# The scatters of the last tokens' list entries placed behind the second early slot's list read and gathers on GpSimd

## Chip, cores, metric

One core of one Trainium2 chip. The metric is device microseconds of one execution, the median over runs.

## What is computed

Three stages on 4608 tokens of 512 values: packed attention (32 pack rows attend to each sequence, then the queries attend to the packs), a mixture of 8 experts in which every token goes to one expert, and a dense two-layer MLP. The part that this change touches is the second:

```python
e_idx = np.argmax(logits, axis=1)
for e in range(E):
    mask = e_idx == e
    h = np.maximum(x[mask] @ w1[e], 0.0)
    out[mask] = gate_w[mask, None] * (h @ w2[e])
```

## The kernel before

**Stages.** The program has two parts, each an order of instructions that a small planner (`Sched`) writes down before anything runs. The first part holds the attention of four batch pairs and, overlapped with its end, the first two expert slots and the fetching of the third slot's rows; the second part (behind a branch, line 1917) holds the third to tenth slot and the nine blocks of the dense MLP.

**Tokens to lists.** When a batch pair's attention output is done, `route` (line 755 on) stores the rows to the DRAM tensor `xs` (lines 806 and 809, on SyncE's queue), chooses an expert for each token on VectorE, and writes the token numbers into per-expert lists in the DRAM tensor `lst`. That write is `send` and `scatter`: per group of 128 tokens one indirect DMA on GpSimd (line 157, `lst<-ids,idx`) with a small memset ahead of it (line 156). A pair has 9 groups. The fourth and last pair is routed in three pieces of 4, 4 and 1 groups; these nine are the "scatters of the last tokens".

**Slots.** A slot is up to 470 tokens of one expert. The first two slots are "early": the first is filled from the tokens of the first two pairs, the second from those of the first three, so neither needs the last pair's list entries. `whole_gather` fills a slot: a list read on SyncE (line 1529, `tok<-lst`), then four indirect gathers on GpSimd (line 1532, `nat<-xs,tok`) into a buffer `nat` of which there is one. `whole_rows` transposes that buffer on TensorE in four sets of four (line 1551, `ft<-ident,nat`), and ScalarE and VectorE split each set into two parts (lines 1556 and 1559). `slot` then runs 8 weight chunks, each a first matmul of 12 pieces (line 1366, `h<-xT,war`) and a second of 12 (line 1674, `o<-g,wbr`). A chunk's weights are loaded by SyncE into one of two `raw` buffers (lines 1417 and 1421) and split on ScalarE (line 1441) and VectorE (line 1447) into a ring of three.

The third slot is an ordinary one and needs every list entry. Its number comes from `finalize` on VectorE (lines 1225 to 1270), its list read and gathers stand in the same two lines, and `slot_list` (line 1583, `st<-lst`) reads the fourth slot's list just behind.

**What sets the order.** `Sched.run` walks through time with estimated durations and always emits the instruction that could start first, by priority where several could. Each engine executes its instructions in the order of emission. The Tile framework adds the semaphores: a read of `lst` waits for every scatter emitted ahead of it, and a scatter emitted behind a read waits for that read. In the trace below "the first group" of gathers are the four of the first early slot, "the second" those of the second early slot, "the third" those of the third slot.

Of the kernel before, what the change touches and what calls it, by code (L numbers as in the profile page):

```python
# [28 lines left out]
NJ = 9  # L29
# [19 lines left out]
class Sched:  # L49
# [12 lines left out]
    def add(self, eng, dur, fn, w=(), r=(), hold=(), prio=0.0, lat=None, deps=(), after=0.0):  # L62
        o = Op()
        o.eng, o.dur, o.fn, o.prio, o.end, o.after = eng, dur, fn, prio, None, after
        o.lat = self.LAT.get(eng, 170.0) if lat is None else lat
        o.deps = list(deps)
        for b in r:
            o.deps += b.writers
        o.bufs = list({id(b): b for b in (*w, *r, *hold)}.values())
        for b in w:  # L70
            b.writers.append(o)
        for b in o.bufs:
            o.deps += b.gate
            b.left += 1
        self.ops.append(o)
        return o
# [12 lines left out]
    def ready(self, o, t):  # L89
        t = max(t, o.after)  # L90
        for d in o.deps:
            if d.end is None:
                return None
            t = max(t, d.end + d.lat)
        need = {}
        for b in o.bufs:
            if b.t is None:
                g = self.given.setdefault(b.key, [])
                k = len(g) + need.get(b.key, 0)
                if b.fifo and b.i != k:  # L100
                    return None
                need[b.key] = need.get(b.key, 0) + 1
                if k >= b.n:
                    p = g[k - b.n]
                    if p.left:
                        return None
                    t = max(t, p.done + 150.0)
        return t
# [1088 lines left out]
def finalize(tc, c, S, pool, tr, prio):  # L1197
# [67 lines left out]
    def taken():  # L1265
        v.tensor_tensor(sel, c["take"], oh.unsqueeze(1).to_broadcast([P, 3, G]), ALU.mult)
        v.tensor_reduce(res, sel, AX.X, ALU.add)
        v.tensor_scalar(add, slot, float(W), None, ALU.mult)
        v.tensor_copy(c["res"][:, 0:1], res[:, 0:1])
        v.tensor_scalar(c["res"][:, 1:3], res[:, 1:3], add, None, ALU.add)  # L1270
# [11 lines left out]
def pad(tc, ctx, n, **kw):  # L1282

    pool = ctx.enter_context(tc.tile_pool(name=f"pad{n}", bufs=1, **kw))
    pool.tile([P, n // 4], F32, name=f"pad_{n}")


class FFN:
# [354 lines left out]
    def slot(self, i, p0, xT, ereg, ready=(), raws=()):  # L1643
# [3 lines left out]
        step = 24 * MM * W / 512  # L1647
        os = self.outs()
        ws = list(ready)
        for fc in range(len(ws), NC1):  # L1650
            raw = raws[fc] if fc < len(raws) else None
# [220 lines left out]
def first_slot(tc, ctx, pctx, own, S, F, T):  # L1872

    def users(*keys):
        return [o for o in S.ops if any(b.key in keys for b in o.bufs)]

    def main():
        own.close()  # L1880
        pad(tc, ctx, 480, side="right")
        F.open(ctx, ("main",), side="right")
        F.open(ctx, ("ps_h",), side="right")

    def psum():
        pctx.close()
        F.open(ctx, ("ps_o",))

    F.gates["main"] = F.gates["ps_h"] = [S.swap(users(*KV_KEYS), main)]
    xT = F.whole_rows(F.xrows, T - 40000 + SHIFT["T0"])  # L1890
    swap = F.c["psum"]
    swap.fn, swap.deps = psum, users("tr", "sc", "xo")
    F.gates["ps_o"] = F.gates["ps_t"] = [swap]
    F.tr_of = None
    T += SHIFT["T5"]
    F.slot(-1, T, xT, [], raws=F.raws)
    for k, (chosen, F.stores, F.sends) in enumerate(F.later, 2):
        e = F.expert(-k, T - 15000, deps=[chosen])
        xT = F.whole_rows(F.whole_gather(-k, T - 12000, e), T)
        T += PER  # L1900
        F.slot(-k, T, xT, e)
    F.stores, F.sends = F.c["stores"], F.c["sends"]
    tables = finalize(tc, F.c, S, F.tables, F.tr, 20000.0)
    e = F.expert(NMORE, T - 10000, deps=[tables])
    xT = F.whole_rows(F.whole_gather(NMORE, T - 8000, e), T + 5000)
    ready = [F.moe_chunk(NMORE, fc, T + PER + (fc - 3) * 24 * MM, e) for fc in range(2)]
    raws = [F.moe_raw(NMORE, fc, T + PER + (fc - 3) * 24 * MM, e) for fc in (2, 3)]
    e = F.expert(NMORE + 1, T + 25000, deps=[tables])
    return xT, ready, raws, F.slot_list(NMORE + 1, T + 26000, e)


def slots_and_mlp(tc, ctx, F, xT, ready, raws, lists):
    nc, c = tc.nc, F.c
    shift = NE_ * NC1 % RING
# [60 lines left out]
def build(tc, ins, out):  # L1975
    nc = tc.nc
    with ExitStack() as ctx, tc.manual_schedule():
        pool = ctx.enter_context(tc.tile_pool(name="dram", bufs=1, space=DRAM))
        xs = pool.tile([NT, DM], F32, name="xs")
        lst = pool.tile([LIST, 2], I32, name="lst")  # L1980
        order = pool.tile([WIDE, 2], I32, name="order")
        yT = pool.tile([DM, WIDE], F32, name="yT")
        tab = ctx.enter_context(tc.tile_pool(name="tables", bufs=1))
        first = ctx.enter_context(tc.tile_pool(name="first", bufs=1))
        with ExitStack() as actx, ExitStack() as pctx, ExitStack() as own:
            c = constants(tc, actx, tab)
            S = Sched()
            late_constants(tc, c, S, ins, lst)
            F = FFN(tc, c, ins, dict(xs=xs, lst=lst, order=order, yT=yT, out=out), first)
            F.tables, F.later = tab, []  # L1990
            F.open(ctx, ("ps_t",))
            c["ps_t"] = F.ps_t
            attention(
                tc, actx, pctx, own, c, S, ins, xs, lst, lambda *a: early_loads(F, S, *a[:3], tab, a[3]), "x"
            )
            ahead = first_slot(tc, ctx, pctx, own, S, F, 50000.0)
            S.run()
        slots_and_mlp(tc, ctx, F, *ahead)
# [25 lines left out]
```

## Time and profile before

| | |
|---|---|
| median of 3 runs | 1427.32 us (1425.44, 1427.32, 1427.41) |
| the profiled execution's own time | 1420.97 us |
| its span | 1419.2 us |
| mean granted TensorE clock | 0.988 |
| TensorE matmul busy | 1365.7 us (96%) |
| VectorE, ScalarE, GpSimd busy | 723.0, 525.8, 253.6 us |

All positions below are microseconds from the start of that span. "Idle before" is the time an engine had no instruction running just ahead of one, with what ended it. The granted clock is a share of full speed: 1.00 is 2.4 GHz, 0.50 is 1.2 GHz.

### The profile page before, as it was taken

What the parts mean: (1) busy time and instruction counts of PE and PEld (TensorE: products, weight loads), DVE (VectorE), ACT (ScalarE), POOL (GpSimd) and SP (SyncE); (2) the same over time, 40 slices, a digit from 0 to 9 for tenths busy, and PEclk for the clock granted to TensorE, in tenths of its full rate; (3) what the DMA queues carried; (4) which work ended last, traced back from release to release, by engine and by line L of the source; (5) the groups of instructions that cost most, each with busy time, mean ns of one, the idle gap of its engine ahead of it and who ended that gap; (6) DMA issues with size and microseconds to landing.
All of it is one profiled execution on the core that took longest, in us unless ns stands there. A gap on an engine that the chain in (4) does not pass through costs nothing.

```text
span 1419.2 us, 20423 instructions
## 1 busy us (share of the span) xinstructions
PE 1365.7 (96%) x7693; PEld 1140.2 (80%) x7693; DVE 723.0 (51%) x1397; ACT 525.8 (37%) x994; POOL 253.6 (18%) x338
## 2 busy tenths in 40 slices
PE   7999797989999999999999999999999999999997
PEld 5777676878888888888888888888888888888885
DVE  5676862458887977877642423324233242322222
ACT  6777633434444443442322322223232232322221
POOL 1345643214432344000010100101000010100101
PEclk9999899999999999999999999999999999999998
DMA  9998546456555566641220200102011010000000
GB/s 271 242 271 210 117 124 135 140 174 201 177 183 167 167 204 201 206 134 60 74 90 0 75 0 27 49 0 75 0 34 42 1 60 1 23 8 0 30 1 30
DMA packets 151315, 142.08 MB, mean 100 GB/s; under 512 B 40390, under 2 KB 128454, under 8 KB 151206
## 3 DMA queue, kind: packets, MB, share of 16 engines
q1 hardware_dynamic: 137862, 121.37, 29.5%
q0 software_dynamic: 13344, 19.31, 4.4%
q8 instruction: 62, 1.02, 0.3%
q14 instruction: 47, 0.39, 0.1%
HBM read 111.76 MB, written 28.87 MB: 99 GB/s over the span
## 4 chain that ended last, share of the span: by engine, by line
PE 58%; DVE 8%; issue 7%; DMA 4%; POOL 1%; SPq 0%; DVEq 0%; ACT 0%; POOLq 0%; ACTq 0%
PE h L1366 29%; PE o L1799 24%; PE o L1674 5%; DMA raw<-moe_w_in 2%; DMA raw<-moe_w_out 2%; DVE g L1663 1%; DVE wbr L1447 1%; DVE war L1447 1%; DVE two L1621 1%; POOL nat L1599 1%; DVE xT L1630 1%; DVE t L1495 1%; DVE t L1488 1%; POOL out L157 0%; DVE t L1496 0%
## 5 line engine op out<-in xcount | busy, mean ns | idle before, releaser
L1799 PE MATMUL o<-wbc,g 128*128 128x512 f32 x1404 | 337.5, 389 | 0.0
L1366 PE MATMUL h<-xT,wac 128*128 128x512 f32 x1404 | 337.1, 389 | 0.0
L1799 PEld LDWEIGHTS o<-wbc,g 128*128 128x128 f32 x1404 | 263.4, 188 | 55.1 <-DVE g L1794 0.4
L1366 PEld LDWEIGHTS h<-xT,wac 128*128 128x128 f32 x1404 | 263.6, 188 | 54.8
L1366 PE MATMUL h<-xT,war 128*128 128x470 f32 (+1 forms) x1284 | 298.4, 380 | 6.1 <-DVE f_sl L1259 2.9
L1787 DVE SCALAR_TENSOR_TENSOR two<-two,h 128x512 f32<-128x512 f32 x144 | 98.9, 687 | 400.3 <-ACT two L1784 397.4
L1366 PEld LDWEIGHTS h<-xT,war 128*128 128x128 f32 x1284 | 240.8, 189 | 45.0 <-issue 3.6
L1784 ACT ACTIVATE two<-h 128x512 f32<-128x512 f32 x144 | 86.0, 597 | 448.4 <-PE h L1366 442.6
L1674 PE MATMUL o<-g,wbr 128*128 128x470 f32 x960 | 223.0, 380 | 5.6 <-DVE g L1663 5.6
L1674 PEld LDWEIGHTS o<-g,wbr 128*128 128x128 f32 x960 | 181.8, 190 | 32.8 <-DVE g L1663 8.2
L157 POOL DMA_INDIRECT out<-two,tok x36 | 37.3, 1035 | 810.7 <-ACT two L1829 805.3
L1599 POOL DMA_INDIRECT nat<-xs,si x105 | 105.3, 1003 | 211.9 <-DVE si L1586 127.9
L1794 DVE TENSOR_TENSOR g<-two,g 128x512 fp32r<-128x512 f32 x141 | 97.5, 691 | 83.9 <-ACT g L1790 83.1
L1790 ACT CAST g<-two 128x512 fp32r<-128x512 f32 x141 | 87.5, 621 | 101.8 <-DVE two L1787 101.3
L1660 ACT ACTIVATE g<-h 128x470 fp32r<-128x470 f32 x80 | 44.9, 562 | 67.5 <-PE h L1366 67.5
L1799 PE MATMUL o<-wbr,g 128*128 128x512 f32 x288 | 69.2, 389 | 0.0
L1447 DVE TENSOR_TENSOR wbr<-raw,wbr 128x512 fp32r<-128x512 f32 x80 | 57.7, 721 | 15.0 <-ACT wbr L1441 14.9
L1441 ACT CAST wbr<-raw 128x512 fp32r<-128x512 f32 x80 | 49.6, 620 | 39.3 <-PE o L1674 34.6
L1447 DVE TENSOR_TENSOR war<-raw,war 128x512 fp32r<-128x512 f32 x80 | 54.7, 684 | 17.3 <-ACT war L1441 17.3
L1799 PEld LDWEIGHTS o<-wbr,g 128*128 128x128 f32 x288 | 54.1, 188 | 11.2
L1663 DVE SCALAR_TENSOR_TENSOR g<-h,g 128x470 fp32r<-128x470 f32 x80 | 51.2, 641 | 18.2 <-ACT g L1660 18.2
L1441 ACT CAST war<-raw 128x512 fp32r<-128x512 f32 x80 | 49.1, 614 | 15.7 <-DMA raw<-moe_w 10.5
(225 smaller groups left out, 1119.8 us busy)
## 6 DMA issues: line engine op xcount, KB each, us to landing
raw<-moe_w SPq DMA_DIRECT2D x160, 256.0 KB
yT<-two SPq DMA_DIRECT2D x40, 235.0 KB
nat<-yT SPq DMA_DIRECT2D x9, 1024.0 KB
kt<-k SPq DMA_DIRECT2D x16, 512.0 KB
qt<-q SPq DMA_DIRECT2D x16, 512.0 KB
vt<-v SPq DMA_DIRECT2D x16, 512.0 KB
xs<-xr SPq DMA_DIRECT2D x8, 1024.0 KB
raw<-moe_w_in SPq DMA_DIRECT2D x16, 512.0 KB
```

What stands on the lines that cost most here:

```text
L1366: nc.tensor.matmul(h.t[:, 0:n], wa[:, a, kc], x[kc].t[:, b, 0:n], start=(kc == 0 and i == 0), stop=(kc == 3 and i == 2),)
L1441: nc.scalar.copy(d, src(i))
L1447: nc.vector.tensor_tensor(d, src(i), h.bitcast(F32), ALU.subtract)
L1599: nc.gpsimd.indirect_dma_start(self.rows(xg)[:, b], None, xs, bass.IndirectOffsetOnAxis(ap=idx.t[:, b : b + 1], axis=0))
L1660: nc.scalar.activation(g.t[:, 0, 0:W], h.t[:, 0:W], AF.Relu)
L1663: nc.vector.scalar_tensor_tensor(g.t[:, 1, 0:W], h.t[:, 0:W], 0.0, g.t[:, 0, 0:W].bitcast(F32), ALU.max, ALU.subtract,)
L1674: nc.tensor.matmul(os[d].t[:, 0:W], w.t[1][:, a, d * P : (d + 1) * P], g.t[:, b, 0:W], start=(fc == 0 and m == 0), stop=(fc == NC1 - 1 and ...
L1784: nc.scalar.activation(th.t, h.t, AF.Tanh, scale=0.851)
L1787: nc.vector.scalar_tensor_tensor(gf.t, th.t, 1.0, h.t, ALU.add, ALU.mult)
L1790: nc.scalar.copy(part()[:, 0], gf.t)
L1794: nc.vector.tensor_tensor(g[:, 1], gf.t, g[:, 0].bitcast(F32), ALU.subtract)
L1799: nc.tensor.matmul(os[k].t, g[:, a, k * P : (k + 1) * P], w.t[1][:, b], start=(i == 0 and m == 0), stop=(i == n - 1 and m == 2),)
```

## The change

The planner gets a second kind of dependency, `behind`: an operation may not be placed ahead of the end of those listed, without the latency that `deps` adds. In `first_slot`, the last nine scatters (`F.c["sends"][-NJ:]`) get the second early slot's four gathers as such. Only the order is changed: no instruction is added or taken away. Lines of the changed file are 4 higher up to `first_slot`'s list read and 8 higher behind it.

```diff
@@ -63,7 +63,7 @@
-        o.deps = list(deps)
+        o.deps, o.behind = list(deps), ()
@@ -92,6 +92,10 @@
             if d.end is None:
                 return None
             t = max(t, d.end + d.lat)
+        for d in o.behind:
+            if d.end is None:
+                return None
+            t = max(t, d.end)
         need = {}
@@ -1896,7 +1900,11 @@
     for k, (chosen, F.stores, F.sends) in enumerate(F.later, 2):
         e = F.expert(-k, T - 15000, deps=[chosen])
-        xT = F.whole_rows(F.whole_gather(-k, T - 12000, e), T)
+        xg = F.whole_gather(-k, T - 12000, e)
+
+        for o in F.c["sends"][-NJ:]:
+            o.behind = (*o.behind, *xg.writers)
+        xT = F.whole_rows(xg, T)
```

GpSimd around the last scatters, before (`idx_3260`, `idx_3360` and `idx_3416` are the three pieces of the last pair, `nat_3481` is the second early slot, `nat_3718` the third slot; each scatter's memset stands ahead of it). These are the last two of the nine scatters; all nine stand ahead of both groups of gathers:

```order
L157 DMA lst<-ids,idx_3360 37376x2
L156 MEMSET tick 128x1
L157 DMA lst<-ids,idx_3416 37376x2
L1532 DMA nat_3481<-xs,tok_3377 118x512 x4
L1532 DMA nat_3718<-xs,tok_3610 118x512 x4
L1916 TENSOR_LOAD f_tot
```

The same place after the change (`nat_3432` is now the second early slot, `nat_3764` the third slot):

```order
L674 TENSOR_TENSOR A_3051<-A_3051,mx_3052 128x512
L674 TENSOR_TENSOR A_3114<-A_3114,mx_3115 128x128
L1536 DMA nat_3432<-xs,tok_3373 118x512 x4
L160 MEMSET tick 128x1
L161 DMA lst<-ids,idx_3260 37376x2
```

The second group of gathers has passed all nine scatters; the third group still stands behind them.

TensorE at the second early slot's transposes, before (`g_3595` and `g_3640` are chunks of the first slot, `ft_3674` to `ft_3708` the four sets):

```order
L1674 MATMUL o_3354<-g_3595,wbr_6_2987 128x470 x3
L1366 MATMUL h_3652<-xT_3145,war_5_2984 128x470 x3
L1366 MATMUL h_3652<-xT_3155,war_5_2984 128x470 x3
L1366 MATMUL h_3652<-xT_3170,war_5_2984 128x470 x3
L1366 MATMUL h_3652<-xT_3191,war_5_2984 128x470 x3
L1551 MATMUL ft_3674<-ident,nat_3481 128x118 x4
L1551 MATMUL ft_3682<-ident,nat_3481 128x118 x4
L1674 MATMUL o_3327<-g_3640,wbr_7_2989 128x470 x3
```

and after (`g_3583` is the chunk that was `g_3595`, `h_3660` the matmul that was `h_3652`):

```order
L1678 MATMUL o_3340<-g_3583,wbr_6_2987 128x470 x3
L1555 MATMUL ft_3642<-ident,nat_3432 128x118 x4
L1555 MATMUL ft_3648<-ident,nat_3432 128x118 x4
L1678 MATMUL o_3352<-g_3583,wbr_6_2987 128x470 x3
L1370 MATMUL h_3660<-xT_3145,war_5_2984 128x470 x3
L1555 MATMUL ft_3666<-ident,nat_3432 128x118 x4
L1370 MATMUL h_3660<-xT_3155,war_5_2984 128x470 x3
L1555 MATMUL ft_3679<-ident,nat_3432 128x118 x4
```

The first two sets have moved up by one `h` and a quarter of an `o`, the other two stand between the pieces of that `h`.

SyncE around the third slot's list read, before (`tok_3610` is that read, `raw_3600` the chunk loaded ahead of it, `raw_3634` the one behind; the ISA rows set an address):

```order
L1421 DMA raw_3600<-moe_w 128x512
L1529 ISA
L1529 DMA tok_3610<-lst 118x4x2
L1583 ISA
L1583 DMA st_3617<-lst 32x30
```

and after (`tok_3722` is that read):

```order
L1421 DMA raw_3689<-moe_w 128x4x128
L1425 ISA
L1425 DMA raw_3689<-moe_w 128x512
L1533 ISA
L1533 DMA tok_3722<-lst 118x4x2
L1587 ISA
L1587 DMA st_3728<-lst 32x30
```

The loads of two more chunks, `raw_3623` and `raw_3689` (before: `raw_3634` and `raw_3671`), have passed the read and the four reads of `st`.

The second early slot's own list read keeps its place on SyncE, right behind the last stores to `xs`.

## Rows read from the trace of the kernel before

**Rows 1.** Waits of TensorE from 196 to 287: us in total, times, longest us

```profile
PE ft L1551 <- DMA nat<-xs,tok: 7.5, 2, 4.7
...
PE h L1366 <- DVEq L1917: 2.4, 1, 2.4
```

**Rows 2.** Timeline of TensorE: start us, us, instructions [idle before <-releaser]

```profile
214.37 2.72 PE L1674 MATMUL o<-g,wbr 128*128 128x470 f32 x12
216.93 2.72 PE L1366 MATMUL h<-xT,war 128*128 128x470 f32 x12
224.37 0.47 PE L1551 MATMUL ft<-ident,nat 118*128 118x118 f32 x1 [4.72 <-DMA nat<-xs,tok]
227.64 2.19 PE L1551 MATMUL ft<-ident,nat 118*128 118x118 f32 x7 [2.79 <-DMA nat<-xs,tok]
...
254.31 0.62 PE L1551 MATMUL ft<-ident,nat 118*128 118x118 f32 x4
254.70 2.81 PE L1366 MATMUL h<-xT,war 128*128 128x470 f32 x12
```

**Rows 3.** Timeline of GpSimd, last scatters and second group of gathers

```profile
192.06 0.97 POOL L157 DMA_INDIRECT lst<-ids,idx  x1 [0.18 <-issue]
...
202.42 0.97 POOL L157 DMA_INDIRECT lst<-ids,idx  x1 [9.29 <-DMA tok<-lst]
...
210.07 0.97 POOL L157 DMA_INDIRECT lst<-ids,idx  x1 [0.19 <-issue]
211.34 1.66 POOL L1532 DMA_INDIRECT nat<-xs,tok  x1 [0.30 <-issue]
...
217.20 1.63 POOL L1532 DMA_INDIRECT nat<-xs,tok  x1 [0.30 <-issue]
233.63 1.63 POOL L1532 DMA_INDIRECT nat<-xs,tok  x1 [14.79 <-PE ft L1551]
```

**Rows 4.** Timeline of SyncE's queue: start us, us of issue, transfers

```profile
189.03 2.16 SPq L809 DMA_DIRECT2D xs<-xr  x2
198.79 0.30 SPq L1529 DMA_DIRECT2D tok<-lst  x1
199.35 1.38 SPq L1417 DMA_DIRECT2D raw<-moe_w  x1
...
208.69 0.56 SPq L1417 DMA_DIRECT2D raw<-moe_w  x1
...
222.76 0.30 SPq L1529 DMA_DIRECT2D tok<-lst  x1
...
226.26 0.55 SPq L1417 DMA_DIRECT2D raw<-moe_w  x1
```

**Rows 5.** GpSimd's first group of gathers and the third route's last scatter

```profile
148.81 1.69 POOL L1532 DMA_INDIRECT nat<-xs,tok  x1 [0.19 <-issue]
...
178.45 0.97 POOL L157 DMA_INDIRECT lst<-ids,idx  x1 [0.19 <-issue]
```

**Rows 6.** DMA queues from 194 to 194.5, SyncE's queue: packets, MB, share of 16 engines

```profile
q1 hardware_dynamic: 60, 0.05, 28.9%
```

**Rows 7.** ScalarE's timeline: first weight splits that waited for a chunk's load

```profile
203.15 0.62 ACT L1441 CAST war<-raw 128x512 fp32r<-128x512 f32 x1 [2.87 <-DMA raw<-moe_w]
...
219.53 0.62 ACT L1441 CAST war<-raw 128x512 fp32r<-128x512 f32 x1 [4.40 <-DMA raw<-moe_w]
```

**Rows 8.** Windows: us, busy us (instructions) of PE, PEld, DVE, ACT, POOL, then PEclk, DMA share, GB/s

```profile
148.80:156.40 7.60, 5.53 (x180) 4.76 (x180) 6.86 (x24) 3.98 (x10) 6.65 (x5) 1.00 0.84 220
196.50:204.50 8.00, 5.14 (x23) 4.02 (x23) 7.58 (x35) 1.80 (x3) 1.88 (x3) 0.95 0.35 97
211.30:218.90 7.60, 7.60 (x38) 6.71 (x37) 1.38 (x3) 1.18 (x2) 6.58 (x4) 1.00 0.77 75
225.00:230.00 5.00, 2.25 (x8) 1.80 (x9) 0.53 (x2) 0.69 (x2) 0.00 (x0) 0.50 0.62 188
286.96:1419.20 1132.24, 1115.71 (x4992) 937.38 (x4992) 551.08 (x884) 358.56 (x622) 135.05 (x166) 1.00 0.24 78
```

## The prediction

> **What bounds the kernel now.** TensorE is busy 96% of the span, so the question is where it is not. From the start of the second part to the end it is busy 1115.71 of 1132.24 us [rows 8]: a shift of that start moves the end. The list of TensorE's waits just ahead of it names the largest: 7.5 us for the second early slot's gathers [rows 1]. TensorE's timeline shows what it costs. An `h` of twelve matmuls starts 2.56 us behind an `o` (214.37, 216.93) and so ends its turn near 219.5; then the first transpose waits until 224.37 and the other seven until 227.64, and the granted clock is 0.50, the 1.2 GHz level, in the five microseconds from 225 [rows 2, 8].
>
> Why the gathers are late stands in GpSimd's and SyncE's timelines. The second of the last nine scatters is issued at 192.06; the list read, emitted behind it, waits for it and goes at 198.79; the third scatter waits for that read until 202.42; seven scatters follow, the last at 210.07, and only then does the first gather go, at 211.34 [rows 3, 4]. The slot needs none of those nine scatters. GpSimd's order alone holds it.
>
> **The list read.** In the new order it waits only for scatters of the third route, the last of which ends its issue at 179.4 [rows 5]. A scatter's landing, seen by the reads behind it, takes 5.8 us (193.03 to 198.79) to 11.7 us (211.04 to 222.76) [rows 3, 4]: 191.1 at the latest. SyncE is free at 191.2, behind the stores to `xs` [rows 4]. The read goes at 191.5 and takes 3.6 us (198.79 to 202.42) when nothing else moves: 195.1. It may queue behind the stores, whose packets last until about 194.5 [rows 6]: 198.1. I take 197.
>
> **The gathers.** GpSimd has nothing left ahead of them and `nat` is free, since the first slot's transposes come before 197. The distance from the first gather's issue to the fourth's landing is 16.3 us in the second group (211.34 to 227.64); in the third it is at most 20.7, because the transposes at 254.31 did not wait for gathers begun at 233.63 [rows 2, 3]. From 197 that gives landing at 213.3, and 218.8 with both upper ends. The transposes now stand behind nine of the twelve matmuls of the `o` that starts at 214.37: wanted at 214.37 + 9 × 0.213 = 216.3. So no wait with my value, 2.5 us with both upper ends.
>
> Here a rule of the Trainium skill speaks against the change. In the trace the gathers come to a stretch where VectorE is busy 7.58 of 8.00 us (`finalize`); before, they ran beside 1.38 of 7.60 [rows 8]. But the first group ran beside 6.86 of 7.60 and its first issue took 1.69 us against 1.66 in the second [rows 3, 5, 8]. The Trainium skill, SBUF — State Buffer, section "SBUF: two separate sides", says that GpSimd cannot write the descriptors of its DMAs while VectorE runs an operation that holds their shared port pair. By that rule the gathers would stand still for much of the stretch; by the first group they do not, and the sum keeps the rows. What standing still would cost is the second rival.
>
> **TensorE.** From 214.37 to the third group's transposes at 254.31 are 39.94 us. The work in it is eleven matmuls of twelve pieces (2.56 each, 28.16) and four sets of transposes at 0.39 (254.31 to 254.70): 29.72 [rows 2]. **Recovered: 10.2 us**, waits and low clock together. The chunk load behind the list read (199.35) goes some 2 us earlier as well; that is worth nothing, since the next wait of TensorE in this stretch is the one for the gathers.
>
> **The third slot.** What passes is late elsewhere. The nine scatters now start when the gathers' issues end, 197 + 4 × 1.95 = 204.8, and take 1.275 each ((210.07 − 202.42)/6): issued by 216.3, against 211.0 before [rows 3]. Four waits come with it: the fifth to eighth scatter reuse the gathers' semaphores and wait for their landing (213.3 at the latest of the four, about the eighth's own turn, so nothing). Behind the scatters on GpSimd are the third group's gathers, behind their landing on SyncE the list read, four `st` reads and the chunk load `raw_3745`. Landing after 5.8 to 11.7 gives the read at 222.1 to 228.0. SyncE comes to it no earlier than about 225, since `raw_3689` ahead of it needs a buffer that the split of the load of 208.69 frees, and that split began at 219.53 for its first half [rows 4, 7]. So 225 to 228; list landed 228.6 to 231.6; gathers landed, at 16.3, 244.9 to 247.9, and at 20.7 by 252.3. The transposes now stand one `h` and a quarter of an `o` further down, 3.2 us of work; with 10.2 us recovered TensorE wants them at 254.31 − 10.2 + 3.2 = 247.3. `raw_3745` goes 3.5 us behind the list read (222.76 to 226.26), at 228.5 to 231.5, lands 3.8 us (199.35 to 203.15) to 10.8 us later (208.69 to 219.53) [rows 4, 7], and needs some 1.3 us of splits: 233.6 to 243.6. TensorE wants it for the second slot's third `h`, which stood two times 2.56 us ahead of 254.31: 249.2 − 10.2 = 239.0. Both waits lie between 0 and about 5 us. The middles, near 247 and 238.6, are just in time; I take **1.0 us** for the two together.
>
> **The rest.** The second part's instructions keep their order, and everything in it starts behind the branch, which TensorE reaches when the first part's matmuls are done; its 2.4 us of wait there [rows 1] moves along. Nothing.
>
> **Sum.** −10.2 + 1.0 = **−9.2 us**. The profiled execution took 1420.97, so 1411.8 under the profile. The median of the runs shown is 6.35 above that execution, and I carry the difference over: 1427.32 − 9.2 = **1418.1 us**. About 0.2%, or 2.9 us, is what a measurement of this kernel can tell from no change.
>
> **Rivals.** *The third slot takes half of it back (0.16).* The list read goes at 228, its gathers take 20.7, or `raw_3745` takes 10.8 to land, beside gathers that now run at the same time. For it: the load of 208.69 did take 10.8 with scatters and gathers about. Against it: the load of 199.35 took 3.8 with scatters behind it. A wait for one gives the other time, so they don't add: about 5 us, result −5.2, 1422.1.
>
> *The second group still lands late (0.09).* GpSimd gets its gathers out only where VectorE leaves it room. In the stretch of 196.5 to 204.5 VectorE is idle 0.42 of 8.00 us, so at the worst the first gather goes at 204.5 instead of 197 and the fourth lands at 204.5 + 16.3 = 220.8, 4.5 us behind 216.3. Against: the first group's issues beside a VectorE as busy. The result is −4.7, 1422.6. This is what the page named above would make of it. With a list landed at 198.1 and 20.7 for the gathers, and no such hold, it is 2.5 us of wait and 1420.6.
>
> *No change (0.07).* The branch's wait grows by what was recovered, because another engine reaches the second part late, SyncE behind its chunk loads for instance. Against: those loads wait for buffers that TensorE frees, and TensorE then is 10 us earlier. 1427.3.
>
> *Slower (0.06): the third slot's list becomes the new wait, larger than the old one.* The last scatters now stand behind the gathers' landings. If the fourth gather lands at 218.8, the eighth scatter starts there and the ninth ends 2.5 us later, at 221.3; with a landing that jams twice the 11.7 us, 23.4, the read goes at 244.7 and the gathers land, with 3.6 and 16.3, at 264.6. Wanted at 247.3 + 2.5: 14.8 us of wait, 17.3 with the 2.5, against 10.2 recovered: +7, and 1434. It decides where the third group lands after 257.5, that is 247.3 + 10.2, so where the scatters take over 21 us to land from 216.3. Nothing in the trace took over 11.7.
>
> **Chances and range.** My forecast has 0.62. Faster by over 0.2%: forecast and the first two rivals, 0.62 + 0.16 + 0.09 = 0.87; within it 0.07; slower 0.06. At best all 10.2 come, 1417.1, and the three runs shown differ by 2 us, so the low end is 1415.5. The high end takes in the first two rivals, 1422.1 and 1422.6: 1423.0. Left out are the last two rivals and a rest at either end, some 0.18.
>
> **What would show it.** Right: the second list read goes near 191.5 and the gathers' first issue near 197; TensorE's wait for them is gone and the clock of 225 to 230 is 1.00; the second part starts near 277 to 278 instead of 286.96. The nine scatters start near 205, the third list read goes at 225 to 228, and TensorE's waits at the third group's transposes and at the second slot's early chunks are under 2 us together. Wrong: a first gather issue later than 201, a third list read later than 230, or a start of the second part that moves less than the waits of the first.

## The result and the profile after

| | before | after |
|---|---|---|
| median | 1427.37 us (4 runs, 1425.44 to 1429.25) | 1414.14 us (4 runs, 1409.89 to 1414.68) |
| ratio | | 0.9914, 95% interval 0.9888 to 0.9940 |
| profiled execution, its own time | 1420.97 us | 1414.15 us |
| its span | 1419.2 us | 1412.4 us |
| mean granted TensorE clock | 0.988 | 0.987 |

The change gains 12.3 us by the ratio, 8.6 to 16.0 by its interval. I had forecast 1418.1 us, 9.2 less than before, in a range of 1415.5 to 1423.0: the time fell and TensorE's wait for the gathers is gone, as forecast, but the time lies 1.4 us below the range.

Lines of the changed kernel are 4 higher up to the list read and 8 higher behind it. The list of TensorE's waits from 196 to 287 us, after (us in total, times, longest us), has no wait for the gathers any more, which [rows 1] had at 7.5 us; the one for `finalize` is now the longest:

```profile
PE h L1370 <- DVE f_sl L1263: 4.1, 1, 4.1
PE h L1370 <- DVEq L1925: 2.4, 1, 2.4
```

TensorE's timeline after, at the second early slot's transposes, at the third slot's and at the start of the second part (columns as in [rows 2]):

```profile
219.60 2.09 PE L1678 MATMUL o<-g,wbr 128*128 128x470 f32 x9
221.53 1.10 PE L1555 MATMUL ft<-ident,nat 118*128 118x118 f32 x8
...
223.77 0.62 PE L1555 MATMUL ft<-ident,nat 118*128 118x118 f32 x4
...
252.89 0.63 PE L1555 MATMUL ft<-ident,nat 118*128 118x118 f32 x4
...
282.36 6.94 PE L1370 MATMUL h<-xT,war 128*128 128x470 f32 x24 [2.44 <-DVEq L1925]
```

Eight transposes run in one go behind nine of the `o`'s matmuls, where before one waited 4.72 us and seven 2.79 [rows 2]. GpSimd's timeline after, to be read beside [rows 3]: the first and fourth gather of the second group, the first, sixth and last of the nine scatters, and the first gather of the third group:

```profile
200.17 1.84 POOL L1536 DMA_INDIRECT nat<-xs,tok  x1 [16.95 <-PE o L1678]
...
206.24 1.64 POOL L1536 DMA_INDIRECT nat<-xs,tok  x1 [0.30 <-issue]
208.18 1.00 POOL L161 DMA_INDIRECT lst<-ids,idx  x1 [0.18 <-DVE f_oh L1267]
...
215.03 0.96 POOL L161 DMA_INDIRECT lst<-ids,idx  x1 [0.19 <-issue]
...
218.99 0.97 POOL L161 DMA_INDIRECT lst<-ids,idx  x1 [0.19 <-issue]
234.01 1.66 POOL L1536 DMA_INDIRECT nat<-xs,tok  x1 [14.05 <-issue]
```

and SyncE's, the second and the third list read, beside [rows 4]:

```profile
194.97 1.14 SPq L1533 DMA_DIRECT2D tok<-lst  x1
...
230.05 0.29 SPq L1533 DMA_DIRECT2D tok<-lst  x1
```

The windows after, with the columns of [rows 8]: the stretch of `finalize`, the five microseconds in which the clock had been 0.50, and the second part.

```profile
200.25:214.25 14.00, 9.93 (x37) 8.36 (x37) 9.96 (x36) 2.36 (x4) 12.14 (x14) 0.76 0.55 139
225.00:230.00 5.00, 5.00 (x27) 4.46 (x26) 2.46 (x5) 1.95 (x4) 0.00 (x0) 1.00 0.43 72
282.36:1412.40 1130.04, 1115.37 (x4992) 937.33 (x4992) 550.36 (x884) 358.43 (x622) 135.19 (x166) 1.00 0.24 78
```

From 225 to 230 TensorE is busy throughout at full clock. The second part's matmuls are the same 4992 with the same busy time within 0.34 us, yet the part is 2.20 us shorter: a gain that no step of mine holds. In this execution everything around 190 us also stands some 3.4 us later than before; that is taken up below, and positions are compared from a mark rather than from the start.

### The profile page after: what moved, and what is told of

Same layout as the page of the kernel before. It is cut to its first block, busy times and chain, and to the rows that moved or that the text cites. A ratio compares the mean times of both kernels' runs of the same rounds, so it can differ in the third digit from the quotient of the medians.

```text
span 1412.4 us, 20422 instructions
## 1 busy us (share of the span) xinstructions
PE 1367.2 (97%) x7693; PEld 1142.4 (81%) x7693; DVE 722.1 (51%) x1397; ACT 526.2 (37%) x994; POOL 252.9 (18%) x338
## 4 chain that ended last, share of the span: by engine, by line
PE 49%; issue 18%; DVE 6%; DMA 4%; POOL 1%; SPq 0%; ACT 0%; DVEq 0%; POOLq 0%; ACTq 0%
PE h L1370 24%; PE o L1803 21%; PE o L1678 4%; DMA raw<-moe_w_in 2%; DMA raw<-moe_w_out 1%; POOL nat L1603 1%; DVE g L1667 1%; DVE war L1451 1%; DVE wbr L1451 1%; DVE two L1625 1%; DMA out<-two,tok 1%; DVE xT L1634 0%; DVE t L1499 0%; POOL out L161 0%; DVE t L1492 0%
```

## Experiments

**Where the time went: both kernels, profiled again.** No edit. Three theories stood against each other: the profiled execution of before waited less than is usual (A), the surplus is spread between executions (B), the second part became shorter as well (C).

> The kernel before, once more, unedited, for a second trace and for the spread. Three theories of why the change gained 12.3 us where the stretch of the wait accounts for 9.8 in the two profiled executions. A: the profiled execution of before had a short wait for the second group of gathers, and a usual one waits longer: this trace then shows over 10 us of TensorE's wait for nat instead of 7.5, and a second part as long as in the first trace (1132 us). B: executions of before differ elsewhere, in the attention stage or the second part, and the wait is the same: 7 to 8.5 us here, with the span's difference outside 196 to 287. C: the change also shortens the second part: it takes 1132 here again against 1130 or less in each trace of the changed kernel. Time against before: ratio 1.000 within 0.003 by all three.

> The changed kernel once more, unedited. A and B: ratio 0.991 to 0.994 against before on the same chip; no wait for nat in this trace; from the twelve o matmuls ahead of the second slot's transposes to the start of the second part 62.8 us, as in the first trace. B: the start of that stretch varies by 1 to 4 us from trace to trace. C: second part 1130 us or less again.

> The changed kernel a third time, as the measure for the three kernels beside it and to see what repeats. In the two profiles so far the way from the `o` ahead of the second early slot's transposes to the second part was 62.8 us, against 72.6 in the profile of the kernel before. Theory A (the profiled kernel before showed a shorter wait for the gathers than is usual): here again no wait for the second group, 62 to 64 us for that way, a second part of 1130 to 1133 us, median 1413 to 1416, ratio to the kernel before 0.990 to 0.994. Theory B (the surplus over 9.2 us is the spread of the executions): the median comes out at 1416 to 1419.

> The kernel before, one more profile, to see which stretch makes its usual time longer than the execution that was profiled first. Three stretches: from the start to the fourth pair's first rank matmul (189.15 and 189.54 in its two profiles so far; 189.3 to 194.0 in those of the changed kernel, whose order is the same up to there), from the `o` ahead of the second early slot's transposes to the second part (72.6 in the first), the second part (1132.2 and 1133.0; 1130.0 to 1130.8 in the changed kernel). Theory A: TensorE's wait for the second group is 9 to 12 us, as the 10.5 of the second profile, and the middle stretch 74 to 77. Theory B: the first stretch takes 192 to 194, as it did in some executions of the changed kernel, the wait is near 7.5. Theory C: wait near 7.5 and first stretch near 189, second part 1134 to 1136.

> The same kernel once more, a fourth execution. The theories expect what they expect of the one beside it; where two of the three stretches are long by turns, the surplus is spread and no single term holds it.

> The kernel before, profiled beside the changed one on one chip. The two profiles taken last had it at 1486.7 and 1483.7 us, with TensorE waiting for instructions in many places, and say nothing of the surplus. If this execution is an ordinary one: theory A expects TensorE's wait for the second group at 9 to 12 us and 74 to 77 us from the `o` ahead of its transposes to the second part; theory B a first stretch (to the fourth pair's first rank matmul) of 192 to 194; theory C a second part of 1133 to 1136.

> The changed kernel on the same chip. Theories A and C: no wait for the second group, 62 to 63 us from that `o` to the second part, as in three profiles before. Theory C: a second part of 1130 to 1131 again. Theory B: a first stretch anywhere from 189 to 194, whichever kernel it is. [...]

Measured: the kernel before against itself 0.9997 (0.9973 to 1.0020) and 0.9996 (0.9974 to 1.0017); the changed kernel 0.9923 (0.9898 to 0.9949), 0.9930 (0.9903 to 0.9958) and 0.9932 (0.9909 to 0.9956). Two profiles of before (e8, e9) have spans of 1486.7 and 1483.7 us: on that chip TensorE stood idle for "issue" (nothing in the profile explains the idle time), up to 7.4 us at one `o`, where in the first profile this comes to 0.7 us in all, so I leave their stretches out. The seven others, cut at four marks of the trace (the fourth pair's first rank matmul, line 819; the `o` ahead of the second early slot's transposes; the first `h` of the second part; the issue of the last scatter to `out`), in us:

| | start to rank | rank to `o` | `o` to second part | to last scatter | to the end |
|---|---|---|---|---|---|
| before | 189.15 | 25.22 | 72.59 | 1123.21 | 9.03 |
| before, e0 | 189.54 | 23.65 | 76.73 | 1123.86 | 9.12 |
| before, e10 | 194.06 | 25.18 | 73.27 | 1123.90 | 9.09 |
| after | 192.59 | 27.01 | 62.76 | 1122.87 | 7.17 |
| after, e1 | 193.96 | 26.46 | 62.42 | 1122.96 | 7.20 |
| after, e7 | 189.34 | 27.68 | 62.38 | 1123.60 | 7.20 |
| after, e11 | 195.15 | 26.43 | 62.26 | 1123.63 | 7.23 |
| mean, after less before | +1.84 | +2.21 | -11.74 | -0.39 | -1.88 |

The first column differs by 5 to 6 us between executions of either kernel, and up to that mark the engines' order is the same but for one memset of 0.09 us on GpSimd; five of the kernels below, with the same order up to there, lie at 189.7 to 193.9. I take it for spread, not for the change. The other four sum to -11.8 us, 0.9917 as a ratio, inside all four intervals. Theory A holds in part: TensorE's waits for the second group in before are 7.5, 10.5 and 7.4 us, and the stretch around them varies by 4 us where the changed kernel's varies by 0.5. B holds for the first column. C holds for the end alone: two columns I had at nothing, +2.2 and -1.9, are systematic. From the mark to the second part the two columns come to -9.5 together.

**The +2.2 us: gathers beside `finalize`.** TensorE's wait for `f_sl` is 2.9 us in every ordinary profile of before and 4.1 in every one of the changed kernel. VectorE's timeline, two of `finalize`'s instructions in before

```profile
199.52 0.17 DVE L1240 TENSOR_SCALAR f_cs<-f_cs 128x16 f32<-128x16 f32 x1
...
201.09 0.22 DVE L1254 TENSOR_SCALAR f_par<-f_cs 128x8 f32<-128x8 f32 x1
```

and the same two after:

```profile
202.97 1.03 DVE L1244 TENSOR_SCALAR f_cs<-f_cs 128x16 f32<-128x16 f32 x1
...
204.82 1.11 DVE L1258 TENSOR_SCALAR f_par<-f_cs 128x8 f32<-128x8 f32 x1
```

The second and the third gather of the group on GpSimd, after:

```profile
202.32 1.69 POOL L1536 DMA_INDIRECT nat<-xs,tok  x1 [0.30 <-issue]
204.31 1.63 POOL L1536 DMA_INDIRECT nat<-xs,tok  x1 [0.30 <-issue]
```

Each of the two instructions takes 0.9 us longer, and each ends with the gather in whose issue it started: 204.00 and 205.93 beside 204.01 and 205.94. The other three profiles of the changed kernel have the same ends to 0.02 us. Between the two, a two-input operation of 128x64 keeps its time (0.22 us before, 0.21 after). Overlaps taken off, the way from `f_left` to the end of `take<-take,p_less` is 4.79 us in before (196.99 to 201.78) and 6.01 after (200.44 to 206.45): 1.2 us, the growth of TensorE's wait; 0.9 of it is at `f_par`. The Trainium skill, SBUF — State Buffer, section "SBUF: two separate sides", calls the port pair that VectorE and GpSimd share an exclusive lock: of an instruction of GpSimd and one of VectorE in a 2-port mode (or with two inputs in SBUF, against a GpSimd instruction that reads SBUF), whichever starts first keeps it to its end and the other is blocked. I had weighed the half in which GpSimd is shut out. These rows agree with the other half, though no view says which mode an instruction of VectorE runs in; the first gather's issue grew by 0.2 us only (1.84 against 1.66 [rows 3]). One row doesn't fit a hold from a gather's first moment: with four scatters ahead (below), `f_ce` starts 0.06 us behind a gather and keeps its 0.23 us.

The remaining 1.0 of the 2.2 us is in the 24 matmuls right behind the wait, in which TensorE is never idle. They take 6.77, 5.19 and 6.73 us in the three profiles of before, at a granted clock of 0.75, 1.00 and 0.75, and 7.34, 6.78, 8.01 and 6.75 us in the four of the changed kernel, at 0.68, 0.75, 0.62 and 0.75: 1.0 us more in the mean, behind the longer idle time.

In the four kernels below that put scatters ahead of the gathers, the gathers are issued behind the part of `finalize` that TensorE waits for; there `f_par` takes 0.22 us again and the wait is 2.8 to 2.9. So it is the gathers' place that makes the 1.2 us.

**Must all nine scatters be passed?** The second list read passes all of them (without that the others wait for it); then nine, eight, six or four stand between it and the gathers:

```diff
-        for o in F.c["sends"][-NJ:]:
-            o.behind = (*o.behind, *xg.writers)
+        for i, o in enumerate(F.c["sends"][-NJ:]):
+            o.behind = (*o.behind, *(xg.writers[0].deps if i < 4 else xg.writers))
```

(`xg.writers[0].deps` holds the list read. This is the edit of e3; in e12 and e13 8 and 6 stand for the 4, and e2 has `xg.writers[0].deps` for all nine.)

> Only the list read passes the nine scatters; the gathers stay behind all of them (the scatters are put behind what the gathers wait for, not behind the gathers). If GpSimd's order holds the gathers, the scatters no longer wait 9.3 us for the list read, start near 197 to 200 and end near 208 to 211 instead of 211.0, so the gathers go 0 to 3 us earlier than before and TensorE's wait stays at 4 to 9 us: ratio 0.996 to 1.000. If the list read is what holds them, nearly the whole gain is here: 0.991 to 0.994.

> The list read first, then the four scatters of the last pair's first piece, then the gathers, then the other five scatters: the gathers 4 x 1.28 = 5.1 us later than in the changed kernel. The changed kernel's gathers began at 200.2 and TensorE reached the transposes at 221.5; at 16.3 us from first issue to last landing that is 5.0 us of slack. So 0 to 2 us of wait and a time within 2 us of the changed kernel: ratio 0.991 to 0.995. If landing takes longer than the 16.3 (20 us), a wait of 3 to 5 us comes back: 0.994 to 0.997.

> Eight of the nine scatters stand between the second list read and its gathers, one behind the gathers. GpSimd's closing DRAIN, behind the last scatter to `out`, took 8.46 us in every profile of the kernel before and of the one where all nine stand ahead of both groups, and 6.58 us in every profile of the changed kernel and of the one with four ahead and five behind. Theory O: any scatter between the two groups of gathers shortens it, 6.58 here. Theory T: it takes a number of them, 8.46 here. In either case TensorE waits for the second group as in the kernel before or nearly (5 to 9 us), VectorE's `f_par` takes 0.22 us because no gather is issued beside `finalize`, and the ratio is 0.995 to 1.000, by 1.9 us lower under O than under T.

> The same with six ahead and three behind. Theory O: a DRAIN of 6.58. Theory T: 8.46 or 6.58, with the number that decides between four and nine. TensorE's wait for the second group 4 to 8 us, ratio 0.995 to 1.000.

| ahead of the gathers | ratio to before (interval) | wait for the second group | GpSimd's closing DRAIN |
|---|---|---|---|
| before (nine, and the list read behind two) | | 7.4 to 10.5 us | 8.46 us |
| nine | 0.9968 (0.9947 to 0.9989) | 2.2 us | 8.46 us |
| eight | 0.9954 (0.9928 to 0.9980) | 5.6 us | 7.97 us |
| six | 0.9961 (0.9934 to 0.9988) | 3.6 us | 7.07 us |
| four | 0.9975 (0.9955 to 0.9996) | 4.7 us | 6.58 us |
| none (the change) | 0.9914 to 0.9932 | none | 6.58 us |

Moving the list read alone gives a third to a half of the gain, with a wait of 2.2 us where I had expected 4 to 9; scatters left ahead of the gathers keep the rest away, and the four ratios can't be told apart by their intervals. The DRAIN of the last column, taken up below, is part of these gains: with four ahead it is 1.9 of 3.6 us. (Eight and six ran on a chip where before, too, took 1488 us; their ratios are to before on that chip, and their waits should not be set against the others'.) With four ahead I had forecast 0 to 2 us of wait and got 4.7: TensorE's timeline of that kernel,

```profile
221.81 0.27 PE L1555 MATMUL ft<-ident,nat 118*128 118x118 f32 x1
222.44 0.38 PE L1555 MATMUL ft<-ident,nat 118*128 118x118 f32 x1 [0.36 <-DMA nat<-xs,tok]
223.20 0.38 PE L1555 MATMUL ft<-ident,nat 118*128 118x118 f32 x1 [0.39 <-DMA nat<-xs,tok]
227.57 1.26 PE L1555 MATMUL ft<-ident,nat 118*128 118x118 f32 x5 [3.99 <-DMA nat<-xs,tok]
```

shows the fourth gather landing at 227.57, 20.6 us behind the first's issue at 206.97: the upper bound that I had taken from the third group, not the 16.3. In the stretch from 218 to 223 the chunk loads take most of the engines,

```profile
q1 hardware_dynamic: 633, 0.49, 66.2%
q0 software_dynamic: 459, 0.36, 30.6%
```

(packets, MB, share of 16 engines; q0 holds gathers and scatters). In the changed kernel the gathers' data are through by 216 us, 16 behind the first issue. That the loads are the cause is not shown: in before they took 60.0% of the engines in the group's first five microseconds (211 to 216), and the fourth gather landed after 16.3 all the same. From first issue to last landing the five profiles of before have 15.7 to 17.3 us, nine ahead 16.4, eight 19.4, six 18.6.

**The -1.9 us: GpSimd's closing DRAIN.** The instructions of the program's last line, in before and after (count, ns least/median/most, first and last start):

```profile
L2019 POOLq DRAIN  x3: 46/113/8462, 1409.9 to 1419.0; - x3
```

```profile
L2027 POOLq DRAIN  x3: 46/113/6583, 1405.0 to 1412.2; - x3
```

GpSimd drains 8.46 us behind its last scatter before and 6.58 after, to 0.01 us in every profile of each, also where a program took 60 us more. The data of that last scatter move within 3 us of its issue in both. Both theories that I put to e12 and e13 fell: neither is it any scatter between the two groups of gathers, nor a switch at some number. With 0, 1, 3, 5 and 9 scatters there it is 8.46, 7.97, 7.07, 6.58 and 6.58 us: 0.45 to 0.49 each, until the fourth or fifth. What GpSimd does in that time stays open.

**How much can the third slot bear?** GpSimd writes `tick` 110 times, or 260 times, between the second group and the scatters; the rest of the order stays.

```diff
+        first = F.c["sends"][-NJ]
+
+        def late(fn=first.fn):
+            for _ in range(110):
+                tc.nc.gpsimd.memset(F.c["tick"], 0.0)
+            fn()
+
+        first.fn = late
```

> GpSimd writes a one-element-wide tile 110 times between the second group of gathers and the nine scatters, a delay d of 3 to 10 us that is read from its trace; nothing else moves. It tells how much the third slot has to spare. Theory S (the scatters stand almost too late): in the changed kernel the third group's last gather was issued at 239.9 and transfers took 11.3 us in the median, so they landed near 251.2 and were wanted at 252.9: a delay d costs d minus 1.7 us (1 to 3), seen as TensorE's wait at the third group's transposes or at a late weight chunk behind the third list read. Theory L (the third slot has room): a delay up to 5 us costs under 0.5.

> The same with 260 such writes: d of 8 to 25 us. Theory S: d minus 1.7 us slower than the changed kernel, so a loss against the kernel before from d of about 14 on. Theory L: d minus 5 or less. Either way the third list read moves by d.

The writes took 17.2 and 40.6 us, more than meant. Medians 1423.55 and 1451.24 us beside 1414.54 of the changed kernel on the same chip: 9.0 and 36.7 slower, ratios to before 0.9992 (0.9972 to 1.0011) and 1.0189 (1.0165 to 1.0213). Counted at GpSimd neither theory fits, since 17.2 us of delay cost 9.0: the third list read moved less than the scatters. It stands 37.0 us behind the rank mark in the changed kernel (36.6 to 37.5), 49.5 in e5 and 72.5 in e6, so 12.5 and 35.5 later. The spans counted from that mark grew by 10.9 and 34.8, so 0.6 to 1.6 us of the move were free: theory S, counted at the read. Its waiter was another, though. VectorE's timeline in e5:

```profile
232.71 0.69 DVE L1451 TENSOR_TENSOR wbr<-raw,wbr 128x512 fp32r<-128x512 f32 x1 [1.15 <-ACT wbr L1445]
243.77 0.68 DVE L1590 TENSOR_SCALAR si<-st,quad 128x15 int32<-128x15 int32 x1 [10.37 <-DMA st<-lst]
243.91 0.64 DVE L1667 SCALAR_TENSOR_TENSOR g<-h,g 128x470 fp32r<-128x470 f32 x1
```

and TensorE's waits there:

```profile
PE o L1678 <- DVE g L1667: 4.5, 1, 4.5
...
PE ft L1555 <- DMA nat<-xs,tok: 1.3, 2, 0.9
```

`si`, which turns the fourth slot's list into addresses, waits for the `st` reads behind the third list read, and a chunk's subtraction `g` is queued behind it on VectorE. TensorE waits 4.5 us for that `g` (28.6 in e6), and for the third group's gathers only 1.3. In the changed kernel `si` runs at 235.56, 2.1 us ahead of its `g`.

**Is the wait for `finalize` worth removing?** VectorE takes the third chunk's subtraction ahead of `finalize`:

```diff
+    n = len(S.ops)
     tables = finalize(tc, F.c, S, F.tables, F.tr, 20000.0)
+    for o in S.ops[n:]:
+        o.behind = (F.los[2],) if o.eng == "dve" else ()
```

(`F.los` collects the subtractions of line 1687.)

> VectorE takes the subtraction of the first slot's third chunk ahead of `finalize` instead of behind it; all else as in the changed kernel. There TensorE stood still 4.1 us for it (203.1 to 207.1) and ran at 0.76 of its clock from 200 to 214. If nothing else is near: 4 to 6 us less than the changed kernel, about 1409. If the gathers of the second and third group are the next bound: they land by about 216 and about 251 and are wanted 4 to 5 us sooner than now (217, 248.5), so 0 to 1 us of wait at the second group and 2 to 3 at the third, and 1 to 3 us are left: about 1412. My forecast is the second.

Measured 1414.53 us beside 1414.54, ratio to before 0.9936 (0.9915 to 0.9957): nothing to be told apart from the change alone. The wait for `f_sl`, 4.1 us, is gone and others came in its place, in TensorE's list from 196 to 310:

```profile
PE ft L1555 <- DVE xT L1563: 2.2, 1, 2.2
...
PE ft L1555 <- DMA nat<-xs,tok: 0.9, 1, 0.9
```

My forecast for it, 1 to 3 us, was too high, and its reason holds for the smaller part only. The third group's gathers cost 0.9 us. The 2.2 us are for VectorE's split of transposed rows (`xT`, begun at 220.59), which stands in VectorE's order behind the split of a chunk's weights, and ScalarE waited 5.0 us for that chunk's load, until 218.52. So in this profile the larger of the new waits goes back to a chunk load.

## Why the prediction was wrong, step by step

- **The list read and the gathers: right.** The read goes 2.38 us behind the rank mark (forecast 191.5 less 189.15, 2.35), its list is there 5.2 us later (5.5), and the gathers are through in 16 (16.3). TensorE doesn't wait. That positions came 3.4 us late on the page, the first gather at 200.17 and the third read at 230.05 against the limits of 201 and 230, is the first column's spread. So is most of a sign of being wrong that did come: the second part starts at 282.36 and not at 277 to 278, 4.6 us earlier than before, less than the 7.5 us of waits. Counted from the mark it starts 8.0 us earlier (89.8 us against 97.8), and the next steps say what is missing there.
- **Recovered, 10.2 us: right against the one execution, wrong as a usual value and as the best case.** Against the profiled 72.59 us the changed kernel's mean of 62.46 is 10.1 less. But two more executions of before take 76.73 and 73.27. I let the low end rest on "at best all 10.2 come", and 10.2 was what one execution had lost; the three lose 11.7 in the mean.
- **The third slot, 1.0 us: 0 measured.** Scatters and list read came where I put them (the read 35.9 to 38.9 us behind the mark; measured 36.6 to 37.5), and nothing waited. "Just in time" was right to 1 or 2 us, but I had followed the late list to the gathers and to the chunk load and not to `si` on VectorE, which is the first to be late.
- **VectorE beside the gathers: not in the sum, +2.2 us.** I asked what VectorE does to GpSimd's gathers and kept the rows' answer, nothing; I didn't ask what the gathers do to VectorE, for which TensorE waited 2.9 us there already. With the -11.7 it makes -9.5 us from the mark to the second part beside my -9.2: that these lie so close is luck, an underestimate and an omission that nearly cancel.
- **"The rest. Nothing.": the step that failed.** I put everything from the branch to the end at nothing because its order doesn't change. Of the second part, -0.4 us is spread, but GpSimd's DRAIN at the program's end takes 1.88 us less (6.58 for 8.46). This and the step on 10.2 are what lies below the range: -10.2 with -1.9 would have put its low end near 1413.6. Five orders show that the DRAIN is shorter the more scatters stand between the second and the third group, until the fourth or fifth; why, stays open.
- **The base.** I carried the 6.35 us between the profiled execution and the median over as they were. They are in more than one stretch: of the 6.3 us by which e10's span is longer than the first profile's, 4.9 are in the first column; of e0's 3.7, 2.6 lie between the mark and the second part. The median of three, 1427.32, was itself 0.9 to 2.1 us above the larger sets that ran later (1426.44 of 29 runs, 1425.58 of 18, 1425.22 of 11). By the three later ratios, 0.9923 to 0.9932, that same median would have fallen to 1416.3 to 1417.6, inside the range. The miss of 1.4 us is smaller than the 4.8 us between the fastest and the slowest of the four runs after.

The 4.0 us between 1418.1 and 1414.14 come out as 2.5 (-11.7 for -9.2 in the stretch), 1.9 and 0.4 (the second part), less 2.2 (`finalize`): 2.6; the remaining 1.4 is of the size of the base's error, and nothing here shows that it is that.

The rivals: the third slot's half did not come, nor a late second group, nor a branch wait (1.9 to 2.4 us as before). The slower one named a real limit. Its condition, a third group landed after 257.5, is a list read at 237.6 (less 16.3 and 3.6); in e5 that read went at 239.15 and the whole gain was gone.

## What to carry to other kernels

When work is moved in an engine's order, list what waits for the moved work and also what runs beside it in the new place, in both directions: here the gathers slowed the very VectorE stretch that TensorE was waiting for. Follow a late transfer to every reader, and behind each reader to what is queued on its engine. A wait read from one execution is one sample; before it is made the best case, look at how far the stretch varies, and count stretches from a mark behind the spread.

## What the hardware showed that I had not expected

- Two one-input VectorE operations of 8 and 16 columns that start 0.5 us or more into the issue of an indirect gather (1.63 to 1.88 us) end with that issue, to 0.02 us, and take 1.0 to 1.1 us instead of 0.17 to 0.22. In the kernels whose scatters are issued there instead, they keep their time, and the scatters take longer: 1.30, 1.35 and 1.29 us for the first three of the kernel with nine ahead, 0.97 for the rest.
- GpSimd's closing DRAIN depends on the order of indirect transfers more than 1100 us earlier: 8.46 us down to 6.58.
- The same four gathers take 15.7 to 17.3 us from the first issue to the last landing with all nine scatters ahead of them or none, and 18.6 to 20.6 with four, six or eight ahead; one profile of each of these, cause not found.
